# Another order of the loads on the one DMA queue of a double attention kernel: weights, x of the second problem, and the first K, V and weights

## The chip, the core and the metric

The kernel runs on one core of one Trainium2 chip. Its time is the device time of one launch in microseconds (us); the time before is the median of nine runs. TensorE is called PE, its weight load PEld, VectorE DVE, ScalarE ACT, GpSimd POOL and SyncE SP. SP computes nothing here: it issues DMAs.

## What is computed

Two problems, A and B, of the same shape, each with its own inputs. Their outputs stand side by side in the last dimension.

```python
# x (16, 80, 576); k_cache, v_cache (16, 16, 512, 128); wq (576, 4096); wo (4096, 576), all bf16
q = (x @ wq).reshape(B, Sq, 32, 128).transpose(0, 2, 1, 3)
k, v = jnp.repeat(k_cache, 2, axis=1), jnp.repeat(v_cache, 2, axis=1)
scores = jnp.einsum("bhqd,bhkd->bhqk", q, k) * (128 ** -0.5)
p = softmax(scores, axis=-1)
o = jnp.einsum("bhqk,bhkd->bhqd", p, v)
out = o.transpose(0, 2, 1, 3).reshape(B, Sq, 32 * 128) @ wo
```

## The kernel before, in words

**Units.** A unit U, from 0 to 127, is one batch row with four K/V heads: 512 KB of K and 512 KB of V. Sixteen units, one for each batch row, make an octet (eight query heads). Octets 0 to 3 belong to A (U=0 to 63), octets 4 to 7 to B (U=64 to 127). Four units make a window W. A chunk m is a quarter of the rows of x (320 rows, four batch rows) with the weights of one octet; chunk m serves the units 4m to 4m+3.

**Work of PE for a unit.** Sixteen score matmuls (line 973, in groups of three) take K as the stationary operand; ACT takes the exponential of each group (line 978). Probabilities times V follow for the first 128 of 160 columns (line 1069) and, at the end of a window, for the other 32 (line 1086). V has a column of ones, so that the row sums come out with it; DVE takes the reciprocal and normalises (lines 1106 and 1111). PE transposes the result (line 1130), DVE evicts it (line 1137), and the output projection with wo follows (line 1167). The projection of q for a chunk has a part with 512 rows of wq (line 936) and a part with the last 64 rows, which lie in a tile `wqr` of their own (line 909, called a visit here). Scores run about one unit ahead of the products with V.

**Loads of a unit.** K comes by a transposing DMA into one of five slots of `kT` (line 1006). V comes by a plain DMA into one of three slots of `v_in` (line 1010), and POOL copies it into one of five slots of `v_sb` (line 1013). The first four K come plainly (line 1028) into space of `wo_sb` and `acc`, and PE transposes them (line 1036). x of A is loaded plainly (line 797) and transposed by PE (line 809); x of B comes in four chunks, each by two transposing DMAs, x and its last part (lines 833 and 836).

**Weights.** Each octet has four pieces of wq of 256 KB and one of 128 KB, `wqr` (lines 869 and 870), and four pieces of wo of 288 KB (line 880). wq, wqr and wo have two slots each, used by turns. Results are stored from `osb` (line 1206): A's while B has already begun.

**What sets the order.** There is no loop that runs at run time. Every instruction gets a key, a number on a common scale, and `_Sched.finalize` (line 85) sorts all of them by key. The order of each engine's instructions is that of their keys, and the semaphore waits follow from the tiles that they read and write. 16 on the scale is one unit, 64 one window. `slot(n)` (line 740) is a place on SP's queue just behind V of the units 2n and 2n+1 and ahead of K of the units 2n+2 and 2n+3. Nearly all DMAs are issued by SP, so its order is one queue: a K pair, a V pair, then what has been given that slot. The keys stand in tables:

- `X_T`, `K_T`, `V_T`, `W1_T`, `WO_T` (lines 647 to 662): the first x, K, V, wq of octet 1 and wo of octet 0; other K and V follow from `KVP`.
- `tw` (line 875): wq pieces of octet g, in the slots 8(g-1)+0, 1, 2, 3 and, for wqr, 3.
- `t = slot(8 * goct - 2 + pc)` (line 883): wo pieces of octet g, in the slots 8g-2 to 8g+1.
- `XB_T` (line 663, used in line 841): the four chunks of B's x, behind K of the units 52, 56, 60 and 64 and the one after each.
- `VS_T`, `Q_T`, `OP_T`, `TX_T`: PE's keys for the first visits, the projections of chunks 1 to 7, the first output projections and the transposes of A's x.

Of the kernel before, what the change touches and what calls it, by code (L numbers as in the profile page):

```python
# [618 lines left out]
def bass_concat_heads__gqa_block_cached__gqa_block_cached__near_ridge_kernel(  # L619
# [18 lines left out]
    NH8 = NSU // 8  # L638
# [5 lines left out]
    PVB = (3, 4)  # L644
    XG = ((0, 3), (3, 5), (5, 8), (8, 10))
    XB = (((0, 3),), ((0, 3), (1, 2)), ((2, 3),), ((2, 3), (3, 2)))
    X_T = (-801.0, -800.0, -796.0, -794.0)
    K_T = (-798.0, -794.0, -60.0, -790.0, -3.0, 2.5)
    KVP = (-46.0, -32.5)
    V_T = (-797.1, -792.0, -58.0, -34.0)  # L650
    WO_T = (1.2, 1.3, 33.2, 33.3)
    VS_T = (-97.2, -62.0, -48.0, -2.3)
    VS_W = (1, 2, 3, 5)
    VIS = set(VS_W) | set(range(6, NW - 2))
    Q_T = ((-56.0, 1.5), (-45.0, 1.5), (27.0, 3.9), (166.3, 5.0), (200.3, 8.5), (264.3, 11.0), (401.3, 8.5))
    QR_T = (7.0, 19.5, 24.0, 36.0, 49.0)
    RB = {"A": 0, "B": QN, "C": 2 * QN, "E": 3 * QN, "D": 4 * QN}
    OP_T = (80.0, 10.5)
    W1_T = (-20.0, -19.9, 1.5, 1.6, 1.7)
    XB_T = (786.8, 850.8, 914.8, 978.8)  # L660
    WQ0 = ((0, 256), (256, 512), (512, 1024))
    JB = (5, 6, 7)
    NKP = 4
    TX_T = (-100.0, -91.0, -57.0, -12.0)
    TK_T = ((-67.0, 2.5), (-11.0, 2.0), (-11.0, 6.0), (17.0, 1.0))
    T_PV0, T_PV1, T_PVL = 4.0, 3.9, (-6.0, -2.0, -1.2)

# [42 lines left out]
    def R(res, ver):  # L710
        return (res, ver)
# [28 lines left out]
    def slot(n):  # L740
        return 32.0 * n - 31.5
# [51 lines left out]
    for g, (t0, t1) in enumerate(XG):  # L793
# [5 lines left out]
        xinr = [R(("acc", 2 + t_ // 2, t_ % 2), ("x", g)) for t_ in range(t0, t1)]  # L799
        add("sp", X_T[g], em_ldz, writes=xinr, dsem="d_x%d" % g, name="ldz%d" % g)  # L800
        parts = ((4, 5), (0, 2), (2, 4)) if nt == 3 else ((4, 5), (0, 4))
        for part, (k0, k1) in enumerate(parts):
# [20 lines left out]
            if k0 == 4:  # L823
                evs.append(("dve", 0.0, em_xdup, [], [R(("xT", c, g, len(parts)), c) for c in cs_], "dup"))
            job(TX_T[g] + 0.3 * part, em_tx, xinr + [IDENT], "tx%d.%d" % (g, part), ("X", g, part), evs)

    for xb in range(4, 8):
        c = xb - 4
        x_ap = probs[1][0].rearrange("b s d -> (b s) d")[c * QN:(c + 1) * QN, :]
        sl = xb % NX  # L830

        def em_ldx(e, x_ap=x_ap, sl=sl):
            return e.dma_start_transpose(xT[:, 0:4, sl * QN:(sl + 1) * QN], x_ap[:, 0:512].rearrange("n (c d) -> n c d", d=128))

        def em_ldx2(e, x_ap=x_ap, sl=sl):
            return e.dma_start_transpose(xT[:, 4, sl * QN:(sl + 1) * QN], x_ap[:, D - 128:D])

        def em_xdup(e, sl=sl):
            return e.copy(xT[0:64, 4, sl * QN:(sl + 1) * QN], xT[64:128, 4, sl * QN:(sl + 1) * QN])

        t = XB_T[c]
        add("sp", t, em_ldx, writes=[R(("xT", sl, "B", 0), xb)] + [R(r_, xb) for r_ in xsub(sl, False)],
            dsem="d_x%d" % sl, name="ldx%d" % xb)
        add("sp", t + 0.1, em_ldx2, writes=[R(("xT", sl, "B", 1), xb)] + [R(r_, xb) for r_ in xsub(sl, True)], dsem="d_x%d" % sl, name="ldx%db" % xb)
        add("act", 64.0 * (14 + c) + 44.0, em_xdup, reads=[R(("xT", sl, "B", 1), xb)], writes=[R(("xT", sl, "B", 2), xb)], name="xdup%d" % xb)

    for goct in range(2 * NOCT):
        prob, q = divmod(goct, NOCT)
        wq_ap, wo_ap = probs[prob][3][:, q * 1024:(q + 1) * 1024], probs[prob][4][q * 1024:(q + 1) * 1024, :]
        sl = goct % 2  # L850
        if goct == 0:
            for hf, (n0, n1) in enumerate(WQ0):
                def em_a(e, wq_ap=wq_ap, n0=n0, n1=n1):
                    return e.dma_start(wq_sb[:, 0, 0:4, n0:n1], wq_ap[0:512, n0:n1].rearrange("(c p) n -> p c n", p=128))

                add("act" if hf == 1 else "sp", (-800.4, -800.5, -799.2)[hf], em_a, writes=[R(("wi", hf), 0)],
                    dsem="d_wi%d" % hf, name="ldwa0.%d" % hf)

            for h in range(2):
                def em_b(e, wq_ap=wq_ap, h=h):  # L860
                    return e.dma_start(wqr[64 * h:64 * h + 64, 0, :].rearrange("p (a n) -> p a n", a=2),
                                       wq_ap[512:576, :].rearrange("p (a h n) -> p a h n", a=2, h=2)[:, :, h, :])

                add("sp" if h else "act", -800.7 + 0.1 * h, em_b, writes=[R(("wi", 3, h), 0)], dsem="d_wi3", name="ldwb0%d" % h)
        else:
            for ck in range(5):
                def em_w(e, wq_ap=wq_ap, sl=sl, ck=ck):
                    if ck < 4:
                        return e.dma_start(wq_sb[:, sl, ck, :], wq_ap[128 * ck:128 * ck + 128, :])
                    return e.dma_start(wqr[:, sl, :], wq_ap[512:576, :].rearrange("p (h n) -> h p n", h=2))  # L870

                wr = [R(("wq", sl, ck), goct)]
                if goct == 2:
                    wr += [R(("wi", hf), 1) for hf in range(3)] + [R(("wi", 3, h_), 1) for h_ in range(2)] if ck == 0 else []
                tw = slot(8 * (goct - 1) + min(ck, 3)) + 0.1 * ck if goct > 1 else W1_T[ck]
                add("sp", tw, em_w,
                    writes=wr, dsem="d_wq%d" % sl, name="ldw%d.%d" % (goct, ck))
        for pc in range(4):
            def em_wo(e, wo_ap=wo_ap, sl=sl, pc=pc):
                return e.dma_start(wo_sb[:, sl, 2 * pc:2 * pc + 2, :],  # L880
                                   wo_ap[256 * pc:256 * pc + 256, :].rearrange("(h p) n -> p h n", p=128))

            t = slot(8 * goct - 2 + pc)
            add("sp", t if goct else WO_T[pc], em_wo, writes=[R(("wo", sl, pc), goct)], dsem="d_wo%d" % sl,
                name="ldwo%d.%d" % (goct, pc))

    for m in range(2 * NOCT * 4):
        goct, c = divmod(m, 4)
# [5 lines left out]
        if m < 4:  # L894
            tv, tx_ = VS_T[m], (2.0, 2.0, 2.0) if m == 0 else (0.5, 0.5, 0.5)
        else:
# [22 lines left out]
        for i in range(8):  # L919
            g, s_ = divmod(i, 2)  # L920
            inpl = role[i] in "XYZ"
            if inpl:
                t = tv + sum(tx_[:"XYZ".index(role[i]) + 1])
            elif m == 0:
                t = -90.0 + 2.0 * nxt
            elif m < 8:
                t = Q_T[m - 1][0] + Q_T[m - 1][1] * nxt
            else:
                t = 64.0 * (m - 1) + QR_T[nxt]
# [33 lines left out]
    for n in range(NGRP):  # L963
        ts = [t for t in range(3 * n, min(3 * n + 3, NCH))]
# [33 lines left out]
    for U in range(NSU):  # L998
# [15 lines left out]

        t_k = K_T[U] if U < len(K_T) else 32.0 * (U // 2) + 0.5 * (U % 2) + KVP[0]
        t_p = T0 - ((18.0, 13.0, 16.0, 22.0)[U % 4] if U > 3 else 40.0)
        t_v = V_T[U] if U < len(V_T) else 32.0 * (U // 2) + 0.5 * (U % 2) + KVP[1]
        if U < NKP:
# [41 lines left out]
    for W in range(NW):  # L1060
# [57 lines left out]
        for u in range(5):  # L1118
# [3 lines left out]
            t = (tmain(W, 3 * lastf + 2) if lastf < 5 else 64.0 * W + 66.0) + (9.5 if u < 3 else 7.5) + (1.5 if u == 4 else 0.0)  # L1122
            h8 = W // 2
# [26 lines left out]
    for h8 in range(NH8):  # L1150
        goct, hb = divmod(h8, 2)
        prob, q = divmod(goct, NOCT)
        osl2, wsl = h8 % 2, goct % 2
        for n in range(10):
            ti, ch = divmod(n, 2)
            r = 5 * hb + ti
            t = (128.0 * h8 + 64.0 + 64.0 * (n // 5) + (3.0, 16.0, 29.0, 43.0, 57.0)[n % 5] if h8 else OP_T[0] + OP_T[1] * n)
            if h8 == NH8 - 1:
                t = 64.0 * (NW - 1) + LAST_T[n]
# [34 lines left out]
            if q == NOCT - 1 and (ch == 1 or last):  # L1194
                rds = [R(("osb", osl, k_), (prob, r)) for k_ in ((ch,) if last else range(2))]
                c0, c1 = (ch * DC, (ch + 1) * DC) if last else (0, D)
                for pi in range(2 if ti < 4 else 1):
                    if ti < 4:
                        dst = out[8 * hb + 2 * ti + pi, 0:64, prob * D + c0:prob * D + c1]
                        src = osb[64 * pi:64 * pi + 64, osl, c0:c1]  # L1200
                    else:
                        dst = out[8 * hb:8 * hb + 8, 64:SQ, prob * D + c0:prob * D + c1]
                        src = osb[:, osl, c0:c1]

                    def em_st(e, dst=dst, src=src):
                        return e.dma_start(dst, src)

                    se = "act" if last and ti == 3 and pi else "sp"
                    ts = slot(int((t + 4.0 + 31.0) // 32.0) + 1) + 0.6 if h8 < NH8 - 1 else None
                    stores.setdefault("op%d.%d" % (h8, n), []).append(  # L1210
                        (se, em_st, rds, "d_out%d" % osl, "st%d.%d.%d" % (prob, r, pi), ts))

# [5 lines left out]
    while jobs:  # L1218
        key, _, emit, reads, name, ver, evac, slot = jobs.pop(0)
# [185 lines left out]
```

## Time and profile before

| | |
|---|---|
| median of 9 runs | 691.99 us |
| lowest and highest | 688.64 and 694.77 us |
| the profiled execution: its time | 689.42 us |
| the profiled execution: its span | 687.7 us |
| granted clock of TensorE, mean | 0.995 |
| issues by SP of K as a transposing DMA | 60 for A, 64 for B |
| issues by SP of V | 64 for A, 64 for B |
| HBM read and written | 89.55 MB and 2.95 MB |

A page of the profile tells of one execution. In its list of engines each entry is the busy time in us, its share of the span and the number of instructions. The row of digits for DMA is the busy share of the DMA engines in tenths, for 40 equal slices of the span. In the list of waits each row names who waited for whom, then the total in us, the number of times and the longest. In the chain of work a row has its start, its length and what it was. In a timeline a row has start, length, engine, line, operation and tiles, and how many instructions were merged. A DMA lands when the last count of its semaphore has come; the trace records these counts apart from the issue.

### The profile page before, as it was taken

What the parts mean: (1) busy time and instruction counts of PE and PEld (TensorE: products, weight loads), DVE (VectorE), ACT (ScalarE), POOL (GpSimd) and SP (SyncE); (2) the same over time, 40 slices, a digit from 0 to 9 for tenths busy, and PEclk for the clock granted to TensorE, in tenths of its full rate; (3) what the DMA queues carried; (4) which work ended last, traced back from release to release, by engine and by line L of the source; (5) the groups of instructions that cost most, each with busy time, mean ns of one, the idle gap of its engine ahead of it and who ended that gap; (6) DMA issues with size and microseconds to landing.
All of it is one profiled execution on the core that took longest, in us unless ns stands there. A gap on an engine that the chain in (4) does not pass through costs nothing.

```text
span 687.7 us, 21766 instructions
## 1 busy us (share of the span) xinstructions
PE 669.5 (97%) x9535; PEld 575.9 (84%) x9535; DVE 415.8 (60%) x1063; ACT 431.7 (63%) x830; POOL 241.1 (35%) x135
## 2 busy tenths in 40 slices
PE   8899999999999999999998899999999999999997
PEld 4698888888888888888777788888888888888896
DVE  4664555556666666666465455556666666666665
ACT  4587766656666666666555666766666666666662
POOL 1324433344233434223423244243434423344340
PEclk9999999999999999999999999999999999999999
DMA  9899999999999999999999999999999999998961
GB/s 290 244 224 217 259 271 260 182 246 269 253 237 216 250 258 238 210 213 215 262 234 255 207 246 261 242 229 237 249 255 242 241 242 254 247 246 217 220 160 47
DMA packets 354633, 160.62 MB, mean 234 GB/s; under 512 B 268390, under 2 KB 350950, under 8 KB 354534
## 3 DMA queue, kind: packets, MB, share of 16 engines
q1 hardware_dynamic: 353702, 158.78, 104.6%
q8 instruction: 76, 1.25, 0.7%
q10 hardware_dynamic: 832, 0.40, 0.2%
q14 instruction: 23, 0.19, 0.1%
HBM read 89.55 MB, written 2.95 MB: 135 GB/s over the span
## 4 chain that ended last, share of the span: by engine, by line
PE 88%; issue 4%; DMA 4%; POOL 2%; ACT 1%; DVE 1%; SPq 0%; POOLq 0%
PE ps L1167 21%; PE ps L936 19%; PE ps L973 19%; PE ps L1069 16%; PE ps L1130 5%; PE ps L1086 5%; PE ps L909 3%; POOL v_sb L1013 2%; DMA kT<-in_A_k_cache_dram 2%; DMA kT<-in_B_k_cache_dram 1%; DMA v_in<-in_A_v_cache_dram 1%; PE ps L770 1%; PE ps L809 0%; DVE qT L944 0%; ACT P L978 0%
## 5 line engine op out<-in xcount | busy, mean ns | idle before, releaser
L978 ACT ACTIVATE P<-ps 128x480 bf16<-128x480 f32 (+1 forms) x683 | 362.7, 571 | 207.6 <-PE ps L973 203.2
L1013 POOL COPY v_sb<-v_in 128x2048 bf16<-128x2048 bf16 x128 | 240.2, 1896 | 427.5 <-DMA v_in<-in_A_v_cache_dram 164.7
L973 PE MATMUL ps<-qT,kT 128*128 128x160 bf16 x2048 | 245.1, 233 | 6.0 <-DMA kT<-in_B_k_cache_dram 3.3
L1069 PE MATMUL ps<-v_sb,P 128*128 128x130 bf16 x2048 | 199.6, 221 | 3.1 <-POOL v_sb L1013 3.1
L973 PEld LDWEIGHTS ps<-qT,kT 128*128 128x128 bf16 x2048 | 161.5, 98 | 22.3 <-issue 6.1
L936 PE MATMUL ps<-xT,wq_sb 128*128 128x320 bf16 x1024 | 173.4, 299 | 1.3 <-ACT rb L1233 1.3
L1069 PEld LDWEIGHTS ps<-v_sb,P 128*128 128x128 bf16 x2048 | 146.7, 98 | 11.1 <-POOL v_sb L1013 3.9
L1167 PE MATMUL ps<-wo_sb,oM 128*128 128x288 bf16 x1024 | 147.1, 287 | 0.6 <-DVE osb L1189 0.6
L1111 DVE TENSOR_TENSOR o_sb<-ps,rinv 128x384 bf16<-128x384 f32 (+1 forms) x224 | 120.6, 539 | 7.7
L936 PEld LDWEIGHTS ps<-xT,wq_sb 128*128 128x128 bf16 x1024 | 91.7, 98 | 29.0 <-DVE rb L1239 1.6
L1167 PEld LDWEIGHTS ps<-wo_sb,oM 128*128 128x128 bf16 x1024 | 96.2, 98 | 20.3 <-DVE osb L1189 0.8
L944 DVE TENSOR_TENSOR qT<-ps,rb 128x320 bf16<-128x320 f32 x160 | 82.7, 517 | 47.8 <-PE ps L936 46.6
L1137 DVE COPY oM<-ps 128x512 bf16<-128x512 bf16 x128 | 54.1, 423 | 57.0 <-PE ps L1130 54.6
L1184 DVE TENSOR_TENSOR acc<-ps,acc 128x288 f32<-128x288 f32 x80 | 36.6, 458 | 68.2 <-PE ps L1167 68.2
L1130 PE MATMUL ps<-ident,o_sb 128*128 128x128 bf16 x640 | 60.3, 220 | 0.1
L1106 DVE RECIPROCAL rinv<-ps 128x3 f32<-128x3 f32 (+1 forms) x224 | 39.1, 175 | 25.7 <-PE ps L1069 14.5
L1233 ACT COPY rb<-ps 128x512 f32<-128x512 f32 (+1 forms) x96 | 48.4, 579 | 9.4 <-PE ps L909 9.4
L945 DVE CAST qT<-ps 128x320 bf16<-128x320 f32 x95 | 49.1, 517 | 8.2 <-PE ps L936 3.9
L1130 PEld LDWEIGHTS ps<-ident,o_sb 128*128 128x128 bf16 x640 | 44.4, 98 | 1.6 <-DVE osb L1189 0.3
L1189 DVE TENSOR_TENSOR osb<-ps,acc 128x288 bf16<-128x288 f32 x40 | 18.3, 457 | 34.3 <-PE ps L1167 27.7
L1167 PE MATMUL ps<-wo_sb,oR 128*128 128x288 bf16 x256 | 37.3, 290 | 0.0
L1086 PE MATMUL ps<-v_sb,P 128*32 128x130 bf16 x2048 | 36.4, 223 | 0.0
(40 smaller groups left out, 178.4 us busy)
## 6 DMA issues: line engine op xcount, KB each, us to landing
v_in<-in_A_v_cache_dram SPq DMA_DIRECT2D x64, 512.0 KB, 5.0
v_in<-in_B_v_cache_dram SPq DMA_DIRECT2D x64, 512.0 KB, 5.1
wo_sb<-in_A_wo_dram SPq DMA_DIRECT2D x16, 288.0 KB, 5.3
wo_sb<-in_B_wo_dram SPq DMA_DIRECT2D x16, 288.0 KB, 5.5
wq_sb<-in_B_wq_dram SPq DMA_DIRECT2D x16, 256.0 KB
wq_sb<-in_A_wq_dram SPq DMA_DIRECT2D x13, 256.0 KB, 5.9
out_dram<-osb SPq DMA_DIRECT2D x32, 72.0 KB, 5.3
wo_sb<-in_A_k_cache_dram SPq DMA_DIRECT2D x2, 512.0 KB, 8.1
```

Source lines behind the costliest of these rows:

```text
L936: last = e.matmul(ps[:, bank, 0:QN], lhsT=wq_sb[:, wsl, ck, i * 128:(i + 1) * 128], rhs=xT[:, ck, xsl * QN:(xsl + 1) * QN], start=(ck == 0 ...
L944: return e.tensor_tensor(dst, src, rb[:, RB[r_]:RB[r_] + QN].rearrange("p (b s) -> p b s", b=4), AluOpType.add)
L945: return e.copy(dst, src) if ev == "act" else e.tensor_copy(dst, src)
L973: last = e.matmul(ps[:, sbk, c * 160:(c + 1) * 160], lhsT=kT[:, U % NK, j, g * 128:(g + 1) * 128], rhs=qT[:, (U // 4) % NQ, U % 4, g, :], ...
L978: return e.activation(P[:, psl, 0:k, :], ps[:, sbk, 0:k * 160].rearrange("p (c n) -> p c n", c=k), AF.Exp, scale=SCALE)
L1013: return e.tensor_copy(v_sb[:, vps, :, 0:128], v_in[:, vs, :, :].rearrange("p g (j d) -> p (g j) d", j=4))
L1069: last = e.matmul(ps[:, bank, off:off + OP_], lhsT=pap(16 * U + 4 * g + j, 0, 128), rhs=v_sb[:, vps, 4 * g + j, :], start=(j == 0), stop=( ...
L1086: last = e.matmul(ps[32 * g:32 * g + 32, bank, off:off + OP_], lhsT=pap(16 * U + 4 * g + j, 128, 160), rhs=v_sb[:, U % NVP, 4 * g + j, :], ...
L1111: return e.tensor_tensor(o_sb[:, osl, 0:nt, :], src, sc, AluOpType.mult)
L1130: last = e.transpose(psb[:, bank, 128 * n_:128 * n_ + 128], o_sb[:, F % NOF, pos, :], ident[:])
L1137: return e.tensor_copy(oM[:, osl2, :, 128 * b8:128 * b8 + 128], psb[:, bank, 0:512].rearrange("p (g c) -> p g c", g=4))
L1167: last = e.matmul(ps[:, bank, 0:DC], lhsT=w, rhs=wo_sb[:, wsl, i, ch * DC:(ch + 1) * DC], start=(i == 0), stop=(i == 7))
```

## The change

Only keys change: the order in which the same instructions stand on SP's queue, and, up to about U=27, the places of some visits, projections and output projections on PE, and with them on ACT and DVE. No instruction is added or dropped, and no tile or number of slots changes.

```diff
-    X_T = (-801.0, -800.0, -796.0, -794.0)
-    K_T = (-798.0, -794.0, -60.0, -790.0, -3.0, 2.5)
+    X_T = (-801.0, -800.0, -796.0, -796.5)
+    K_T = (-798.0, -794.0, -794.2, -788.7, -3.0, 10.5)
     KVP = (-46.0, -32.5)
-    V_T = (-797.1, -792.0, -58.0, -34.0)
+    V_T = (-798.4, -792.0, -66.0, -31.0)
...
-    VS_T = (-97.2, -62.0, -48.0, -2.3)
+    VS_T = (-97.2, -62.0, -48.0, 6.7)
...
-    Q_T = ((-56.0, 1.5), (-45.0, 1.5), (27.0, 3.9), (166.3, 5.0), (200.3, 8.5), (264.3, 11.0), (401.3, 8.5))
+    Q_T = ((-56.0, 1.5), (-45.0, 1.5), (27.0, 3.9), (166.3, 5.0), (216.3, 9.0), (264.3, 11.0), (393.3, 8.0))
...
-    OP_T = (80.0, 10.5)
-    W1_T = (-20.0, -19.9, 1.5, 1.6, 1.7)
-    XB_T = (786.8, 850.8, 914.8, 978.8)
+    OP_T = (94.0, 10.5)
+    W1_T = (-59.8, 1.3, 1.5, 1.5, 1.7)
+    WQ_S = {2: (-1, 1, 3, 3, 3), 3: (0, 2, 3, 3, 3), 4: (3, 4, 4, 4, 6), 5: (3, 3, 4, 5, 5), 6: (-1, 1, 3, 3, 5)}
+    WO_S = {1: (-2, -1, 0, 1), 2: (-2, 0, 0, 1), 3: (-3, -3, 0, 0), 4: (-4, -1, -1, -1), 5: (0, 0, 0, 1)}
+    XB_S = (26, 30, 32, 33)
+    ST_S = {6: 0, 7: 0}
...
-    TX_T = (-100.0, -91.0, -57.0, -12.0)
+    TX_T = (-110.0, -83.0, -57.0, -12.0)
...
-        t = XB_T[c]
+        t = 32.0 * XB_S[c] - 45.2
...
-                tw = slot(8 * (goct - 1) + min(ck, 3)) + 0.1 * ck if goct > 1 else W1_T[ck]
+                tw = slot(8 * (goct - 1) + WQ_S.get(goct, (0, 1, 2, 3, 3))[ck]) + 0.1 * ck if goct > 1 else W1_T[ck]
...
-            t = slot(8 * goct - 2 + pc)
+            t = slot(8 * goct + WO_S.get(goct, (-2, -1, 0, 1))[pc]) + 0.01 * pc
```

The resulting order on SP's queue around the passage from A to B, one K pair to a line (x0 is the first chunk of B's x with its last part; wq4.1 is the second wq piece of octet 4; st are stores). First before:

```
k52 k53 x0 v52 v53 wq4.2
k54 k55 v54 v55 wq4.3 wqr4
k56 k57 x1 v56 v57 st st
k58 k59 v58 v59 st st
k60 k61 x2 v60 v61 wo4.0 st st
k62 k63 v62 v63 wo4.1 st st st
k64 k65 x3 v64 v65 wo4.2 wq5.0 st st
k66 k67 v66 v67 wo4.3 wq5.1 st st
k68 k69 v68 v69 wq5.2 st st
k70 k71 v70 v71 wq5.3 wqr5 st st st
k72 k73 v72 v73
k74 k75 v74 v75
```

and after:

```
k52 k53 x0 v52 v53
k54 k55 v54 v55 wq4.0
k56 k57 v56 v57 wo4.0 wq4.1 wq4.2 wq4.3 st st
k58 k59 v58 v59 st st
k60 k61 x1 v60 v61 wqr4 st st
k62 k63 v62 v63 wo4.1 wo4.2 wo4.3 st st st
k64 k65 x2 v64 v65 st st
k66 k67 x3 v66 v67 st st
k68 k69 v68 v69 st st
k70 k71 v70 v71 wq5.0 wq5.1 st st st
k72 k73 v72 v73 wq5.2
k74 k75 v74 v75 wq5.3 wqr5
```

In octet 2 the first wq piece moves one slot earlier and the third one slot later; in octet 3 the second and third move one slot later. Of octet 2 one wo piece moves one slot later, of octet 3 three pieces move one or two slots earlier (wo3.0 and wo3.1 stand behind V43, wo3.2 and wo3.3 behind V49). In octet 6 wq6.0 stands behind V79, wq6.2 and wq6.3 behind V87 and wqr6 behind V91, instead of behind V81, V85, V87 and V87. wo of octet 5 stands with three pieces behind V81 and one behind V83, instead of one piece behind each of V77, V79, V81 and V83. Octet 7, both wo and wq, stays.

At the very beginning V0 comes ahead of K0, the last two loads of A's x change places and come ahead of K1, K2 comes ahead of K1, and the second wq piece of octet 1 goes behind K4 and the first wo pieces. K5 still follows wqr of octet 1. On PE four of the projections of chunk 0 that stood behind the transposes of x's second part come ahead of them, and the visit of chunk 3 comes after three more groups of scores.

More of the change, by code (lines that the diff above doesn't have):

```diff
@@ L1208, in bass_concat_heads__gqa_block_cached__gqa_block_cached__near_ridge_kernel @@
                     se = "act" if last and ti == 3 and pi else "sp"
-                    ts = slot(int((t + 4.0 + 31.0) // 32.0) + 1) + 0.6 if h8 < NH8 - 1 else None
+                    ts = slot(int((t + 4.0 + 31.0) // 32.0) + 1 + ST_S.get(h8, 0)) + 0.6 if h8 < NH8 - 1 else None
                     stores.setdefault("op%d.%d" % (h8, n), []).append(
```

## The prediction

> **What bounds the kernel now.** I read the page first, then the waits of PE, the stretches between certain pairs of K, the chain in order of time, and SP's timeline.
>
> ```profile
> PE 669.5 (97%) x9535; PEld 575.9 (84%) x9535; DVE 415.8 (60%) x1063; ACT 431.7 (63%) x830; POOL 241.1 (35%) x135
> DMA  9899999999999999999999999999999999998961
> q1 hardware_dynamic: 353702, 158.78, 104.6%
> ```
>
> PE and DMA look equally full, so shares alone don't decide. PE's waits do:
>
> ```profile
> PE ps L973 <- DMA kT<-in_B_k_cache_dram: 3.3, 2, 2.2
> PE ps L1069 <- POOL v_sb L1013: 3.1, 3, 2.6
> PE ps L973 <- DMA kT<-in_A_k_cache_dram: 2.7, 2, 2.0
> ```
>
> Every long wait after the start is for K, or for V through POOL's copy. In the chain:
>
> ```profile
> 126.87 11.42 DMA kT<-in_A_k_cache_dram
> ...
> 364.66 1.91 POOL v_sb L1013
> ...
> 385.83 9.19 DMA kT<-in_B_k_cache_dram
> ```
>
> K24 is issued at 126.87 and lands 11.42 us later; K72 likewise at 395.02. (K24 is K of unit U=24.)
>
> ```profile
> 217.50:302.30 84.80, 84.80 (x1222) 73.86 (x1220) 54.38 (x138) 53.58 (x102) 29.99 (x16) 1.00 1.12 236
> 302.30:395.20 92.90, 85.22 (x1185) 72.13 (x1183) 52.30 (x136) 55.40 (x107) 29.93 (x16) 0.98 1.08 235
> 476.00:557.40 81.40, 81.40 (x1179) 70.81 (x1177) 53.07 (x137) 51.44 (x98) 30.11 (x16) 1.00 1.11 246
> 138.80:142.20 3.40, 3.40 (x25) 2.84 (x23) 0.42 (x1) 1.71 (x3) 0.13 (x1) 0.50 1.06 301
> ```
>
> Columns: stretch, length, busy time by engine, clock, DMA share. From U=56 to 72 (302.3 to 395.2) PE needs 92.9 us; the same 16 units take 81.4 from U=88 to 104. So 11.5 us are lost where A passes to B. The last line is a stretch at half clock after the 2.03 us idle at K24; another (367.5 to 370.9) follows the 2.59 us at V66. Each costs 1.7 us.
>
> Now SP, for the reason:
>
> ```profile
> 27.69 0.67 SPq L870 DMA_DIRECT2D wqr<-in_A_wq_dram  x1
> 34.84 2.31 SPq L1006 DMA_TRANSPOSE kT<-in_A_k_cache_dram  x1
> ...
> 476.13 7.49 SPq L1006 DMA_TRANSPOSE kT<-in_B_k_cache_dram  x2
> 483.67 1.13 SPq L1010 DMA_DIRECT2D v_in<-in_B_v_cache_dram  x2
> 484.84 7.59 SPq L1006 DMA_TRANSPOSE kT<-in_B_k_cache_dram  x2
> ```
>
> SP waits 6.5 us (28.36 to 34.84) for the K slot of U=0. After that no gap above 0.46 us comes before 600: each K's slot was released up to 12 us before its issue. The queue is the limit for 560 us; PE's idle time is only where it shows. A pair without other pieces takes 8.7 us (484.84-476.13); PE takes 81.4/8=10.2.
>
> **What the Trainium skill says.** "Perfetto Trace Analysis", section "DMA Instruction — HWDGE (DVE, Sync)": the profiled time of an issue starts when its semaphores are satisfied and leaves out the movement of data. The trace agrees: gapless SP slices of up to 7.3 us, landing about 5 us after V's issue. "DMA: Bandwidth & Descriptors", section "Why a DMA increments its semaphore by 16 and not by 1": a copy uses only as many engines as divide the slowest dimension of both sides; wqr's source leads with 2. The trace agrees: wqr's 128 KB lands 2.75 us after the piece ahead of it (390.50-387.75), V's 512 KB takes 1.5. "TensorE: Matmul & The Clock Gate", section "What's actually happening": idling can halve the clock, and the free-running window is about 3.4 us; the trace shows 3.4 us at 0.50, but not after the 2.17 us idle at K72.
>
> **Costs on the queue.** From landings of successive K pairs: bare pair 8.75; wo piece +0.5 (9.0, 9.07, 9.8, 9.4); wq piece +1.25 (about 10.0 alone); wqr +2.7 (12.65 with a wq piece); x of one B chunk +3.0 (12.4 with two stores); two stores +0.5. Data of wq alone would be 0.75, of wo 0.8 (landing to landing); I take the pair differences and keep 0.5 per wq piece as the other end.
>
> **The change, part by part.** No transfer and no PE instruction is added or dropped; what changes in order on PE lies before U=28. So the queue's sum stays, and each K or V moves by what stands before it:
>
> *First K, V and weights.* The same DMAs precede K5 (V0 is now ahead of K0, K2 ahead of K1, one wq piece later). K0 lands 1.5 us later, 13.4; its transposes ran at 13.41: no cost, hidden by 16 projection matmuls that moved ahead of them (2.4 us); without cover 1.5 us. But two score groups now precede the visit of chunk 3, which waited 1.04 us: U=0's last score group moves from 34.44 to about 31. K5 then need not wait after wqr (34.17). A K behind wqr lands 3.3 to 3.4 us after it (472.16 to 475.47, 550.72 to 554.15): 37.5 instead of 39.22. The whole queue is 1.75 us earlier. Ends: 0 if that group stays late, 3.7 if the issue decides.
>
> *wq and wo of octets 2 and 3* cancel by K24 and K40. K24: slack 0.14 plus 1.75: its stall and half clock go, PE gains 3.5 us by U=30; next late is wqr of octet 4.
>
> *x1, x2, x3 and weights at the A/B border.* Gain at a unit = slack before + pieces no longer ahead + 1.75:
>
> | unit | slack | moved behind it, net | may gain |
> |---|---|---|---|
> | V60 | 0.06 | x2, wqr less wo: 5.2 | 7.0 |
> | V62 | 0.06 | x2: 3.0 | 4.8 |
> | V64 | 0.06 | x3 less two wo: 2.0 | 3.8 |
> | V66 | 0.06 | wq less wo: 0.75 | 2.6 |
> | K72 | 0.14 | two wq, wqr: 5.2 | 7.1 |
> | K76 | 2.77 | none | 4.5 |
> | K84 | 3.03 | none | 4.8 |
> | K88 | 0.57 | wqr: 2.7 | 5.0 |
> | K92 | 3.50 | none | 5.2 |
> | K104 | 3.32 | none | 5.1 |
>
> Slack is first use less landing (V: less end of copy). The added wait: wqr of octet 4 now stands behind V61. V61 lands at 331.22-5.2-1.75=324.3, wqr at 327.05. The visit of chunk 16 (326.33 before; 322.8 with the 3.5 gained) waits 4.3 us, and scores, PV, then DVE, ACT and POOL's next slots queue behind it. The other moved pieces have time: x1 lands near 320 for chunk 17 (349.3), wqr of octet 5 near 407 for chunk 20 (418.5 less 4.5), wqr of octet 6 near 490 for chunk 24 (500.1 less 4.5). The wait at chunk 16 is covered: V66 holds PE at 366.6-2.6=364.0 anyway, and from the visit PE needs 33.5 (418.51 to 452.17 an octet later), so 360.5, or 362.2 with half clock.
>
> From V66, PE needs 23.9 to K72 (452.17 to 476.05): 387.9, against a landing at 388.1. It needs 20.3 to K76 (476.05 to 496.40): 408.3, where K76 lands at 412.20-1.75=410.45: idle about 2.2, gain 414.97-410.5=4.5. All later units allow more. After K104 PE alone counts. **Sum: 4.4 us off.**
>
> The profiled execution took 689.42, span 687.7 (1.7 around it): 685.0. The median of 9 runs is 691.99, 2.6 higher; against it I predict 687.6.
>
> **Rivals.**
> 1. Bunches are cheaper (22%): wq pieces side by side (three behind V57, two behind V23, V39, V71, V87) cost their data, 0.5 less each; some eight pieces by K76 give up to 4 us, bounded by K84 to K104 and a PE that needs 10.2 a pair: 8 off, 684.0. For it: two stores cost 0.5 together. Against: wo plus wq measure 10.5, about their sum.
> 2. The gain is halved (18%): K5 isn't earlier, or the idle time at K76 is followed by half clock, 1.7 us that no later limit hides: 2.7 off or less, 689.5. For it: two of three such waits before had it.
> 3. Slower (14%): bunches cost more. Place: the slots behind V33, V57, V63, V71, V81, V87, where three to six DMAs delay the next K. Price: one slot with wq and wqr varied from 11.3 to 13.8; 1.25 above the sum at seven slots before K104 is 8.8, less 4.4: 4.4 slower, 696.4. It decides from 0.63 a bunch. Against: pieces have added up so far.
> 4. Nothing gained (6%): PE's earlier arrival meets the same late K later on, 691.5.
>
> **Numbers.** The forecast of 4.4 has 40%. About 0.3% (2.1 us) is what a measurement of this kernel can tell from no change. Faster: 40+22 and two thirds of rival 2, 74%; same: the rest of rival 2, rival 4 and a point of rival 3, 13%; slower: 13%. The range leaves out most of rival 3 and the far end of rival 1: 682.5 to 693.0.
>
> **What would show it.** K5 issued near 31 to 32, landing near 37.5; no wait at K24; PE waiting about 4 us for wqr at chunk 16 near 327; V66 first used near 364; PE idle at K76 near 410; U=56 to 72 about 89 us; SP gapless up to 600. I am wrong if a bare pair no longer takes 8.7, if octets' queue times change by more than 2 us, or if PE waits after K76.

## The result, and the profile after

| | before | after |
|---|---|---|
| median | 691.81 us (54 runs) | 685.06 us (17 runs) |
| lowest and highest | 686.1 and 696.62 us | 681.78 and 688.94 us |
| time of the profiled execution | 689.42 us | 681.77 us |
| its span | 687.7 us | 680.0 us |

The ratio of after to before is 0.9902, with a 95% interval of 0.9885 to 0.992: 6.8 us faster, 5.5 to 8.0. I had forecast 4.4, which lies below that interval and inside the range that I gave. The profiled execution of after was quicker than any of these 17. In after every line number from the tables on is 3 higher.

The page of after, engines, DMA row and queue:

```profile
PE 666.4 (98%) x9535; PEld 573.5 (84%) x9535; DVE 418.2 (61%) x1063; ACT 431.1 (63%) x830; POOL 241.3 (35%) x135
DMA  9999999999999999999999999999999999999961
q1 hardware_dynamic: 353702, 158.78, 106.1%
```

The same packets and bytes as before; the DMA engines are as full. PE's list of waits in after:

```profile
PE ps L976 <- DMA kT<-in_B_k_cache_dram: 1.5, 1, 1.5
...
PE ps L976 <- issue: 1.1, 1, 1.1
PE ps L1072 <- POOL v_sb L1016: 1.0, 1, 1.0
```

Of the 9.1 us that PE waited for K and V before, 2.5 are left, and no wait for `wqr` is there. The chain of waits of after, where PE waits for K76:

```profile
396.95 10.16 DMA kT<-in_B_k_cache_dram
407.11 0.14 issue
407.25 0.37 PE ps L976 x3
```

The stretches from first use to first use, U=40 to 56, 56 to 72 and 88 to 104, of after:

```profile
220.89:302.34 81.45, 81.45 (x1179) 70.86 (x1177) 52.48 (x133) 51.47 (x98) 31.94 (x17) 1.00 1.12 253
302.34:385.81 83.47, 82.31 (x1184) 71.17 (x1182) 52.80 (x136) 54.84 (x107) 28.15 (x15) 1.00 1.09 235
...
468.37:549.79 81.42, 81.42 (x1179) 70.83 (x1177) 53.07 (x137) 51.47 (x98) 30.22 (x16) 1.00 1.12 240
```

U=56 to 72 took 92.90 us before and takes 83.47 in this execution, at a clock of 1.00. K40 and K56 are first used at 220.89 and 302.34, as before (220.93 and 302.36): in this trace all that was gained comes later. SP's timeline of after at the beginning:

```profile
27.68 0.66 SPq L873 DMA_DIRECT2D wqr<-in_A_wq_dram  x1
31.58 3.15 SPq L1009 DMA_TRANSPOSE kT<-in_A_k_cache_dram  x1
```

K5 is issued at 31.58 instead of 34.84 and lands at 36.89 instead of 39.22.

This looks like the prediction's sum with less waiting. But one execution is thin ground: the same kernel profiled again (e11) looks different where it matters. The part on why the prediction was right therefore goes by all fourteen profiles.

### The profile page after: what moved, and what is told of

Its sections match the earlier page's. It is cut to its first block, busy times and chain, and to the rows that moved or that the text cites. A ratio compares the mean times of both kernels' runs of the same rounds, so it can differ in the third digit from the quotient of the medians.

```text
span 680.0 us, 21766 instructions
## 1 busy us (share of the span) xinstructions
PE 666.4 (98%) x9535; PEld 573.5 (84%) x9535; DVE 418.2 (61%) x1063; ACT 431.1 (63%) x830; POOL 241.3 (35%) x135
## 3 DMA queue, kind: packets, MB, share of 16 engines
q8 instruction: 76, 1.25, 0.7%
## 4 chain that ended last, share of the span: by engine, by line
PE 89%; issue 4%; DMA 2%; ACT 2%; POOL 2%; DVE 1%; POOLq 0%
PE ps L1170 21%; PE ps L939 19%; PE ps L976 19%; PE ps L1072 16%; PE ps L1133 5%; PE ps L1089 5%; PE ps L912 3%; POOL v_sb L1016 2%; DMA kT<-in_B_k_cache_dram 1%; ACT P L981 1%; DMA acc<-in_A_x_dram 1%; ACT xT L819 0%; PE ps L812 0%; DVE okm L1291 0%; ACT rb L1236 0%
## 5 line engine op out<-in xcount | busy, mean ns | idle before, releaser
L1140 DVE COPY oM<-ps 128x512 bf16<-128x512 bf16 x128 | 54.2, 423 | 52.3 <-PE ps L1133 49.8
```

The source lines that it names most:

```text
L1140: return e.tensor_copy(oM[:, osl2, :, 128 * b8:128 * b8 + 128], psb[:, bank, 0:512].rearrange("p (g c) -> p g c", g=4))
```

## The experiments

e1 to e4 ran on one chip, e5 to e8 on a second, e9 to e12 on a third; on these the kernel before had medians of 694.82, 696.52 and 695.21 us. Ratios are to the kernel before on the same chip, with a 95% interval.

**e1, the beginning alone.** The tables of the beginning as after; weights, x as before.

```diff
+    WQ_S = {}
+    WO_S = {}
+    XB_S = (26, 28, 30, 32)
```

> The changed beginning alone (first K, V, wq and the order on PE up to about U=27); all later places on the queue as before. Theory Q (the queue's running sum decides; K5 lands 2.3 us earlier in the changed kernel): the whole queue is about 2 us earlier, so K72 and K76, which PE has to wait for, allow 2 us: 1.5 to 3 us faster than before. Rival H (the beginning makes the whole gain): 6 to 7 us faster. Rival W (the head start is lost again where PE itself runs later in the first octets): 0 to 1 us.

Measured: ratio 1.0009 (0.9988 to 1.0031), no difference. K5 lands at 36.06, but PE's waits at the A/B border are all still there:

```profile
PE ps L976 <- DMA kT<-in_B_k_cache_dram: 6.8, 3, 3.5
PE ps L1072 <- POOL v_sb L1016: 2.9, 4, 1.2
PE ps L976 <- issue: 2.3, 1, 2.3
```

The 3.5 us are at K72, and 6.8 us at half clock go with them. The 2.3 us that the list calls issue, idle time for which it shows no cause, stand at U=23 (137.2), and 3.4 us at half clock go with them. Theory Q, 1.5 to 3 us faster, did not come; rival W's 0 to 1 us did. In this profile PE reaches K76 5.9 us after it has landed, so an earlier K76 could not help. But an earlier queue should also have eased the wait at K72, and why it didn't isn't shown.

**e2, all but the beginning.**

```diff
-    V_T = (-798.4, -792.0, -66.0, -31.0)
+    V_T = (-797.1, -792.0, -58.0, -34.0)
...
-    W1_T = (-59.8, 1.3, 1.5, 1.5, 1.7)
+    W1_T = (-20.0, -19.9, 1.5, 1.6, 1.7)
```

(and `X_T`, `K_T`, `VS_T`, `Q_T`, `OP_T`, `TX_T` likewise as before).

> The change without its beginning: all later places on the queue (x, weights of octets 2 to 6) as in the changed kernel. Theory Q with the sums of the prediction: 2.7 us faster than before (K76 binds with its slack of 2.8). If the trace of the changed kernel is typical, where the head start is gone by U=40 and the queue between K48 and K76 is 5.4 us shorter, 6 to 7 us faster, as the whole change. Rival H: no gain.

Measured: ratio 0.994 (0.9918 to 0.9962). PE's waits:

```profile
PE ps L912 <- DMA wqr<-in_B_wq_dram: 7.4, 1, 7.4
PE ps L976 <- DMA kT<-in_A_k_cache_dram: 2.8, 2, 1.7
```

The new wait that I predicted at the visit of chunk 16 is real, and longer than my 4.3 us. Some six tenths of the whole gain (0.6%, with an interval of 0.4% to 0.8%, of 1.0%) come without the beginning. That lies between the two sizes that theory Q named, 2.7 and 6 to 7 us.

**e3, x of B alone.** Beginning and weights as before, `XB_S` as after.

> Only the four loads of B's x stand at their new places; beginning and weights as before. Theory Q: V66 still has all four x and the same weights ahead of it, and K76 as well, so 0 to 1 us faster. Rival X (x loads cost about 1 us less each when no weight piece stands in the same slot, as the two traces suggest): no weight has moved here, x1 to x3 still stand beside stores, x2 beside no wo; 2 to 4 us faster only if the new neighbours matter.

Measured: 0.9991 (0.9966 to 1.0016), no difference. PE waits 5.0 us at V66 and 3.1 at K72: with the weights unmoved the same pieces still stand ahead of K72.

**e4, the weights of octets 4 and 5 alone.**

```diff
+    WQ_S = {4: (3, 4, 4, 4, 6), 5: (3, 3, 4, 5, 5)}
+    WO_S = {3: (-3, -3, 0, 0), 4: (-4, -1, -1, -1)}
+    XB_S = (26, 28, 30, 32)
```

> Only the weights of octets 4 and 5 stand at their new places; beginning, x and the other octets as before. Theory Q: V66 gains 0.8, K72 5.2, K76 has its slack of 2.8: 2 to 3 us faster than before. Rival B (bunched pieces cost less than single ones): 5 us or more faster. Rival C (bunches cost more): slower than before.

Measured: 0.997 (0.9946 to 0.9994). It waits 7.2 us for `wqr` at chunk 16, as e2; no wait at K72, 0.6 at K76. The gain, 2.1 us (0.4 to 3.8), fits the 2 to 3 of theory Q. Of the three parts run alone (e1, e3, e4) it is the only one that gains.

**e5, weights of octets 2, 3 and 6 back.** After, with these at the old places.

> The kernel after, with the weight pieces of octets 2, 3 and 6 (and wo of octets 1, 2 and 5) back at their old places; the beginning, x and the weights of octets 4 and 5 stay moved. My theory (additive sum, head start needed at the A/B border): these pieces cancel within their octets, so the time is that of the kernel after within 1 us (ratio to before 0.989 to 0.992) and PE's waits at K76 (about 1.5 us) stay. Rival W (the order of octets 2 and 3 is what keeps K24 and K40 on time once PE is earlier): PE waits 2 us or more at K24, the clock halves there, and the ratio is 0.994 or more.

Measured: 0.9899 (0.9855 to 0.9944). PE waits 1.8 us at K24, with the clock kept, and 7.8 at chunk 16. That these pieces do nothing that can be measured fits the sum. The rival's half clock at K24 didn't come; its 2 us there nearly did, and its ratio of 0.994 lies at the end of the interval. After itself was not run on this chip.

**e6, the bunches spread.**

```diff
-    WQ_S = {2: (-1, 1, 3, 3, 3), 3: (0, 2, 3, 3, 3), 4: (3, 4, 4, 4, 6), 5: (3, 3, 4, 5, 5), 6: (-1, 1, 3, 3, 5)}
+    WQ_S = {2: (-1, 1, 2, 3, 3), 3: (0, 1, 2, 3, 3), 4: (3, 4, 5, 5, 6), 5: (2, 3, 4, 5, 5), 6: (-1, 1, 2, 3, 5)}
-    WO_S = {1: (-2, -1, 0, 1), 2: (-2, 0, 0, 1), 3: (-3, -3, 0, 0), 4: (-4, -1, -1, -1), 5: (0, 0, 0, 1)}
+    WO_S = {1: (-2, -1, 0, 1), 2: (-2, -1, 0, 1), 3: (-4, -3, -2, -1), 4: (-4, -1, 0, 1), 5: (-2, -1, 0, 1)}
```

> The kernel after, with the same weight pieces spread out: no slot has more than two wq pieces, and wo pieces stand in slots of their own. Additive sum: the queue's time per octet is unchanged, so the time is that of the kernel after within 1.5 us. Rival 1 (bunched pieces cost only their data, 0.5 us less each): some eight pieces up to K76 cost up to 4 us more when spread, so 3 to 4 us slower than after. Rival 3 (bunches cost 0.63 us or more each): 4 us faster up to where PE alone limits, so at most 2 to 3 us faster than after.

Measured: 0.9878 (0.9836 to 0.9921), 1.2 us below e5 by medians on that chip. The 3 to 4 us slower of rival 1 are not there; rival 3's 2 to 3 us faster can't be told from this. Additive costs fit, but aren't the only reading that does.

**e7, `wqr` in two DMAs.** After, with

```diff
-                    return e.dma_start(wqr[:, sl, :], wq_ap[512:576, :].rearrange("p (h n) -> h p n", h=2))
+                    return e.dma_start(wqr[0:64, sl, :], wq_ap[512:576, 0:512])
...
+                    return e.dma_start(wqr[64:128, sl, :], wq_ap[512:576, 512:1024])
```

> The kernel after, with each wqr piece (128 KB, one DMA whose source leads with 2 and so runs on 2 engines) cut into two DMAs of 64 partitions each, which use all 16. Same bytes, one DMA more for each octet. If 2 engines are what makes wqr cost 2.7 us on the queue, it falls to about 0.7 us or less, the queue runs about 2 us an octet shorter, the waits at V66, K72 and K76 (1.04, 0.12 and 1.54 us) go, and the kernel is 2.5 to 3 us faster than after, with PE the only bound. If the cost is the switch between kinds of transfer and not the engines, wqr still costs about 2.5 us, with 0.3 us more for the second DMA: no change or 1 us slower.

Measured: 0.9844 (0.9803 to 0.9884): 685.61 us, where e5 and e6 had 689.47 and 688.25 on that chip. PE's waits (lines 5 higher than in after):

```profile
PE ps L917 <- DMA wqr<-in_B_wq_dram: 3.2, 1, 3.2
...
PE ps L1077 <- POOL v_sb L1021: 0.8, 1, 0.8
```

The queue did get shorter: from the landing of K76 to that of K104, with two `wqr` between, the three kernels with the cut took 138.3, 138.7 and 138.8 us, the eleven others 139.9 to 144.5. The mean of the eleven is 142.3, so a `wqr` costs about 1.8 us less, and the second reading, that the switch between kinds is the cost, fails. That agrees with what the Trainium skill says in "DMA: Bandwidth & Descriptors", section "Why a DMA increments its semaphore by 16 and not by 1": a copy is spread only over as many engines, 16 at most, as divide the slowest dimension of both its sides, 2 for the one DMA and 16 for halves of 64 rows. The number of engines itself isn't in these traces. In time the intervals of e6 and e7 overlap.

**e8, the kernel before with `wqr` in two DMAs.**

> The kernel before, its order kept, with only wqr cut into two DMAs of 64 partitions. If the queue's length up to K72 is what the change of order works around, 2 us less for each octet brings K24, V66 and K72 in time: stalls and half clock there go, 7 to 11 us faster than before (ratio 0.984 to 0.990). If order at the A/B border matters and not the length, the waits there stay and the gain is under 3 us.

Measured: 0.9942 (0.9912 to 0.9972), less than the 7 to 11 us of the first theory. The wait at K24 is gone, those of the border aren't: the 8.3 us for V are in five waits from 298.7 to 373.7, 3.4 of them at V66.

```profile
PE ps L1074 <- POOL v_sb L1018: 8.3, 5, 3.4
```

By the ratio the gain is 4.0 us (2.0 to 6.1), between the two theories. So the queue's length counts, but in this profile a shorter queue alone leaves the waits of the border in place.

**e9, `wqr` of octet 4 earlier.** After, with one DMA moved:

```diff
-    WQ_S = {..., 4: (3, 4, 4, 4, 6), ...}
+    WQ_S = {..., 4: (3, 4, 4, 4, 4), ...}
```

> The kernel after, with one DMA moved: wqr of octet 4 goes four pairs back, beside its wq pieces behind V57 instead of behind V61. PE's order is unchanged. My prediction's claim (the new wait for wqr at the visit of chunk 16 is covered, because V66, K72 and K76 are as late as before and PE then waits there): the wait at chunk 16 goes, V66, K72 and K76 land when they did, PE waits for them longer, and the time is that of the kernel after within 1.5 us on the same chip. Rival (the wait is uncovered and costs its length and the half clock behind it): 4 to 10 us faster than after.

Measured: 0.9922 (0.9899 to 0.9946), against 0.991 of e11 on that chip; the medians are 690.57 and 688.04 us. No gain is seen, and the rival's 4 to 10 us are ruled out; whether the time is within 1.5 us of after can't be told. PE's waits of e9, then those of e11:

```profile
PE ps L976 <- DMA kT<-in_A_k_cache_dram: 3.1, 2, 2.0
PE ps L1072 <- POOL v_sb L1016: 2.6, 1, 2.6
PE ps L1170 <- DVE osb L1192: 2.2, 1, 2.2
PE ps L976 <- DMA kT<-in_B_k_cache_dram: 1.9, 2, 1.7
```

```profile
PE ps L912 <- DMA wqr<-in_B_wq_dram: 7.1, 1, 7.1
PE ps L976 <- DMA kT<-in_B_k_cache_dram: 2.6, 2, 1.6
...
PE ps L1072 <- POOL v_sb L1016: 1.2, 1, 1.2
```

A wait of 7.1 us is taken away, and PE makes the visit at 328.71 instead of 332.64. Ahead of the visit there is a new wait of 2.0 us for K58 (315.28), which now stands behind `wqr`; after it PE waits 2.2 for an output tile and 2.6 at V66. V66 is first used at 368.96 (369.69 in e11) and K76 at 415.51 (415.79). The wait for `wqr` was covered, as the prediction claimed.

**e10, both: `wqr` in two DMAs, and that of octet 4 earlier.**

> The kernel after with both: wqr cut into two DMAs of 64 partitions, and wqr of octet 4 beside its wq pieces behind V57. If V66 and K72 cover the wait at chunk 16 (in e7_wqr_two it was 3.24 us, followed by 0.78 at V66, and K72 was first used only 0.27 after landing), this is e7's time within 1 us: about 0.984 of before. If they don't, 3 to 5 us faster than e7: ratio 0.977 to 0.980.

Measured: 0.9899 (0.9852 to 0.9947). No wait at chunk 16; 4.2 us at V66 in its place, which is first used at 363.43 (363.34 in e7). So it is covered here too. But the ratio isn't e7's 0.984, though the intervals overlap: beside e11 on that chip (688.04 us) e10 with 688.05 gains nothing. Whether cutting `wqr` is worth time on top of after stays open; e7's gain was not seen again.

**e11, after again.**

> The kernel after, unchanged, on the chip of these four runs. If the profiled run of after was a quick one (its queue took 189.5 us from K40 to K76, where nine other profiled runs of kernels with the same or nearly the same pieces took 192 to 200), this one's queue takes about 196, PE waits 4 to 8 us for wqr at the visit of chunk 16, and the span is 685 or more. If the order itself makes that stage 5 us shorter, it again takes 189 to 191 and there is no wait for wqr.

Measured: 0.991 (0.988 to 0.994); its profile has a span of 690.3. PE's timeline in e11:

```profile
324.87 0.63 PE L1072 MATMUL ps<-v_sb,P 128*128 128x130 bf16 x8
332.64 1.25 PE L912 MATMUL ps<-xT,wqr 64*128 64x320 bf16 x10 [7.13 <-DMA wqr<-in_B_wq_dram]
```

and the same place in the first profile of after:

```profile
325.75 0.63 PE L1072 MATMUL ps<-v_sb,P 128*128 128x130 bf16 x8
326.31 0.72 PE L912 MATMUL ps<-xT,wqr 64*128 64x320 bf16 x10
```

The ten visit matmuls take 1.25 us instead of 0.72: they lie in a stretch at a clock of 0.50 (330.80 to 337.60) that began while PE stood idle. From the landing of K40 to that of K76 the queue took 198.4 us here, and 189.5 in the first profile, with the same instructions in the same order. U=56 to 72, 83.47 us in the first profile, took 92.78 here, as long as in the profile of before (92.79). The first profile was a quick execution (681.77 us, against a median of 685.06 on its chip); it hid the new wait. This one was a long one (692.06 against 688.04), so neither is typical.

**e12, two of PE's placements back.**

```diff
-    Q_T = (..., (216.3, 9.0), (264.3, 11.0), (393.3, 8.0))
-    OP_T = (94.0, 10.5)
+    Q_T = (..., (200.3, 8.5), (264.3, 11.0), (401.3, 8.5))
+    OP_T = (80.0, 10.5)
```

> The kernel after, with SP's order kept and only two of PE's placements back at the old values: the Q projections of one early chunk and of the last, and the output projection (Q_T's fifth and last pair, OP_T). If PE's new order in the first octets is what costs it the gain there (visit of chunk 5 at 84.5 instead of 83.2), the visit of chunk 5 comes at about 83 and PE is 1 us or more earlier up to K24; with the queue the bound behind that, the time is that of after within 1 us. If PE's order also slows the queue (five runs with the new beginning took 39.3 us from K8 to K16, five with the old one 36.8), that stage falls to about 37 and the kernel is 1 to 2 us faster than after.

Measured: 0.9884 (0.9835 to 0.9933), 2.5 us below e11 by medians, but the intervals overlap. The stretches from the visit of chunk 4 to that of 5, to that of 6, and on to the first use of K24, in e12 and then in after:

```profile
62.43:82.72 20.29, 20.29 (x296) 17.62 (x295) 11.42 (x30) 13.88 (x29) 7.51 (x4) 1.00 1.17 241
82.72:103.01 20.29, 20.29 (x296) 17.63 (x295) 11.46 (x30) 13.82 (x29) 7.51 (x4) 1.00 1.06 248
103.01:135.74 32.73, 32.73 (x510) 29.13 (x508) 18.30 (x49) 22.64 (x46) 13.08 (x7) 1.00 1.11 237
```

```profile
62.93:84.54 21.61, 21.44 (x302) 18.28 (x302) 11.22 (x29) 14.25 (x29) 7.53 (x4) 1.00 1.12 238
84.54:105.24 20.70, 20.47 (x294) 17.51 (x294) 11.45 (x29) 13.91 (x28) 7.53 (x4) 1.00 1.15 245
105.24:139.73 34.49, 33.06 (x509) 29.11 (x508) 18.31 (x49) 22.44 (x45) 13.04 (x7) 1.00 1.12 232
```

The three stretches take 73.3 us in e12 and 76.8 in after. With the old placements PE comes to K24 4.0 us earlier than in the first profile of after and 3.2 earlier than in e11; 1.2 and 1.1 of that are there at the visit of chunk 3 (32.32, 33.54 and 33.44), ahead of the placements that differ. At the visit of chunk 15 it is still 3.4 us ahead of e11 (301.75 and 305.15). The queue from K8 to K16 took 38.4 us. The expectation compared unlike sets: after, e6, e7, e9, e10, e11 and e12 have one wq piece of octet 2 between these two K, which e1 and e5 don't have. The six others of these seven took 39.7 to 42.1 us, and e2, with that piece and PE's old order, 37.4. This points the way of the second half of the expectation; one profile doesn't settle it.

## Why the prediction was right, and where it wasn't

All profiled executions, read at K76 (landing from the semaphore's last count, first use from PE's first score matmul of the unit):

| kernel | K76 lands | used after | wait for `wqr` at chunk 16 | span | span less first use |
|---|---|---|---|---|---|
| before | 412.20 | 2.77 | none | 687.7 | 272.7 |
| e1 | 418.48 | 5.88 | none | 697.5 | 273.1 |
| e3 | 417.35 | 5.12 | none | 695.2 | 272.7 |
| e8 | 417.06 | 2.73 | none | 692.8 | 273.0 |
| e2 | 417.44 | 0.20 | 7.38 | 690.3 | 272.7 |
| e4 | 414.86 | 0.20 | 7.17 | 689.5 | 274.4 |
| e5 | 419.93 | 0.20 | 7.78 | 694.6 | 274.5 |
| e6 | 414.53 | 0.20 | 7.60 | 689.0 | 274.3 |
| after | 407.11 | 0.20 | none | 680.0 | 272.7 |
| e11 (after) | 415.58 | 0.20 | 7.13 | 690.3 | 274.5 |
| e12 | 409.42 | 0.20 | 4.46 | 682.8 | 273.2 |
| e9 | 415.31 | 0.20 | moved | 689.3 | 273.8 |
| e7 | 406.88 | 0.83 | 3.24 | 680.8 | 273.1 |
| e10 | 407.65 | 1.79 | moved | 682.5 | 273.1 |

The four above have the weights of octets 4 and 5 at the old places (e3 with x moved, e8 with `wqr` cut), and PE comes to K76 2.7 to 5.9 us after it has landed. The eight below them, e2 to e9, have them moved and load `wqr` in one DMA: PE stands waiting when K76 lands. (e7 and e10, with a shorter queue, are close to it.) From there the end is 272.7 to 274.5 us away in every kernel. That is the mechanism of the prediction.

- **The queue is the bound up to K76, PE after it: right in the main.** e9 takes 7.1 us of PE's waiting away and the first use of K76 doesn't move. After K76 nothing waits in the first profile. In others a K comes late once more (1.1 and 1.2 us at K88 in e4 and e5, 0.8 and 1.05 at K104 in e6 and e11), which the column on the right shows. A wait of PE after K76 was one of my signs of being wrong, and this is it: the border between the two bounds isn't sharp.
- **K5 need not wait: right in place; what it is worth isn't shown.** It was issued at 31.58, as foreseen. In eight profiles with the new beginning and new placements of PE K5 lands at 36.2 on the mean, in five with the old beginning at 39.5. The lead is 4.1 us at K8 (54.2 and 58.3), but only 0.9 at K16: between them the queue takes 40.0 us instead of 36.8. In part that is one piece more, the first wq piece of octet 2, which the change puts ahead of K16 and which six of the eight have there. After's queue has

```profile
83.15 0.51 SPq L872 DMA_DIRECT2D wq_sb<-in_A_wq_dram  x1
```

  behind V15 and ahead of K16; before's has it behind V17. e1 and e5, without it, take 38.7 and 37.4 us, the four old ones without it 35.6 to 37.7; what is left is open. At K40, with the same transfers ahead, the lead is 1.7, but 0.6 without the three kernels with `wqr` cut. So whether the 1.75 that I carried on arrives at K76 isn't shown. The beginning alone gained nothing (e1); after against e2, which ran on another chip, leaves it 0.3% to 0.4%, with intervals that touch.
- **K24's stall goes and PE gains 3.5 by U=30: the first half right in the profile (in e5 and e9 1.8 and 1.1 us are left), the second wrong.** K40 is first used when it was before. I had costed the new places on PE before U=28 at nothing; by e12 they hold PE up by some 2 to 3 us from the visit of chunk 3 on. In the profiles the queue takes that up: PE waits at K76 in e12 as in after (2.16, 1.54 and 1.55 us). The medians, 2.5 us apart, neither show nor rule out a cost.
- **The new wait for `wqr` of octet 4: right, though the first profile hides it.** It is 7.1 to 7.8 us in e2, e4, e5, e6 and e11 and 4.46 in e12, against my 4.3. It is longer because the queue ran later: V61 was to land at 324.3, and in e11 it landed at 329.48. It is covered by V66, as I said (e9, e10). It goes with how late the queue runs: in the first profile of after V61 landed at 322.46, and there is none.
- **V66 near 364, K72 without a stall, U=56 to 72 in about 89 us: right in place.** V66 was first used at 360.97, in e11 at 369.69, later than the 366.61 of before; PE waited 1.0 and 1.2 us there. K72: 0.12 and none. U=56 to 72 took 83.5 and 92.8, and 89.4 in e12. Single landings differ by more than what was forecast.
- **K76 lands at 410.45, PE idle 2.2, gain 4.5: right in mechanism.** The idle time was 1.5 to 2.2 in after, e6, e9, e11 and e12. The landings scatter from 407 to 420, so the 410.45 can't be judged from one trace.
- **The size.** The term that was too small seems to be the slack at K76. I took 2.77 from the one profile of before, in which the 2.17 us idle at K72 went without half clock. In e1 and e3, with the same weights ahead of K72, the idle was 3.5 and 3.1, half clock went with it, and PE was 5.9 and 5.1 behind. In e1:

```profile
400.60:407.40 6.80, 5.46 (x39) 4.75 (x40) 0.90 (x3) 2.17 (x4) 1.90 (x1) 0.50 0.99 261
```

  The mean of the four (e8 with its cut `wqr` among them) is 4.1; with the 1.75 of the beginning the sum is 5.9, inside the interval of 5.5 to 8.0. This is an account after the fact and not a test: each slack is from one execution, those of e1 and e3 ran 4.7 and 2.1 us above the medians of their kernels, that of before 2.4 below its own, and the 1.75 isn't shown. e2, without the beginning, gains 0.6%, which is 4.1 us of 692 (0.4% to 0.8%), and that agrees with the slack alone. Apart, the parts gain nothing (e1, e3) and 0.3% (e4); together they gain 1.0%, more than their sum.
- **Costs of pieces.** Additive costs fit (e6), and `wqr` in one DMA is the dear piece, as I read it (e7). I had named a change of the queue's times as a sign of being wrong. From K40 to K76, with the same transfers, it took 194.7 us in before and 189.5 and 198.4 in after: one order scatters by 8.9 us, more than any cost in the sum, so single profiles can't test the costs closely.
- **Rivals.** 1 (bunches cheaper, 684.0) gave nearly the measured time for a reason that e6 doesn't show. 2 and 4 lie outside the interval of the measured gain, and so does the forecast of 4.4. 3 would have made after slower than before, and neither measurement of it did.

What stays open: how much of the gain the beginning makes, why the lead shrinks between K8 and K16 by more than the one piece, what makes one execution's queue quicker than another's, and whether cutting `wqr` gains on top of after.

## What to carry to other kernels

When one queue is full, ask for every load how late its consumer stands behind it; where the consumer is late only because an earlier stall pushed it back, moving pieces out from ahead of that stall can gain up to the whole slack, and a new wait upstream of the next late load can be free, as the one of 7 us was here (e9). Size that slack from several executions: here it was 2.8 us in one and 5.9 in another with half clock behind the stall. A single profile can hide a wait of 7 us that the next ones show, so profile the same kernel again before you explain a difference by it.

## What the runs showed that I had not expected

- **One order, two speeds.** After took 189.5 and 198.4 us from K40 to K76 in two executions. In the trace's packet records of that stretch, the 82,670 packets under 512 bytes on the queue have a mean of 24.9 ns in the first and 26.3 in the second (26.0 in before). With the same packets, the packets themselves were longer; over fourteen profiles the two go together loosely (correlation 0.66).
- **Half clock comes in steps.** Stretches at half clock were 3.4, 6.8 or 10.2 us long, multiples of the 3.4 us window that the Trainium skill names in "TensorE: Matmul & The Clock Gate", section "What's actually happening". In e11 one was

```profile
330.80:337.60 6.80, 4.96 (x83) 3.65 (x84) 2.14 (x6) 1.75 (x4) 1.89 (x1) 0.50 0.86 174
```

  beginning within 7.13 us of idle time; within 7.60 (e6) one of 10.2 began. An idle time of 2.02 in e9 was followed by 3.4, one of 2.60 in the same run by none: its length alone doesn't decide.
- **The new places on PE have a price, but not through longer matmuls.** In the three stretches shown at e12 PE is busy for 75.0 us in after (21.44, 20.47 and 33.06) and for 73.3 in e12. That looks like slower matmuls and isn't: records of the same shape are as long in both, to 3%, but after has eight output projections with wo more in these stretches (160 and 152 start there), which e12 makes before them; eight in a row take about 1 us. From the start of the span to the first use of K24 both make the same 1788 matmuls: PE is busy for 132.5 us in after and 131.4 in e12, and idle for 7.2 and 4.3 (e11: 132.8 and 6.2). In after 1.14 us of the idle time are the gap that the list calls issue. Where the other 1.1 us of busy time come from isn't shown.
